# Splitting a vector-matrix product in front of a matmul stage differently: six and two blocks, row form, smaller loads

## The chip, the cores and the metric

The kernel runs on one core of one Trainium2 chip. The metric is the device time of one execution in microseconds (us). Ratios compare the mean time of one kernel's fast runs with that of the other's of the same rounds on the same chip, so they are not quite the ratio of the medians that are quoted. A verdict of faster or slower needs 2%.

## The reference, cut to what matters

The program is one transformer block with conditioning: six vectors come from `silu(c) @ w_mod`, the first two of them (`sa`, a shift, and `ca`, a scale) are needed at once, since they modulate the input of the first projections.

```python
mod = (_silu(c) @ w_mod).reshape(c.shape[0], 6, 1, -1)      # c: 1x1024, w_mod: 1024x6144, bf16
sa, ca, ga, sb, cb, gb = (mod[:, 0], mod[:, 1], ...)         # cut
h = _layernorm(x, axis=-1) * (1 + ca) + sa                   # x: 1x2048x1024
x = x + ga * _A_ref(h, A_wqkv, A_wo)                         # linear attention; k, v, q from h @ wqkv
h = _layernorm(x, axis=-1) * (1 + cb) + sb
x = x + gb * _B_ref(h, B_w_gate, B_w_up, B_w_down)           # gated FFN, F = 3584
```

Of the kernel before, what the change touches and what calls it, by code (L numbers as in the profile page):

```python
# [8 lines left out]
ACT = mybir.ActivationFunctionType  # L9
ALU = mybir.AluOpType  # L10
BF16 = mybir.dt.bfloat16
F32 = mybir.dt.float32
# [9 lines left out]
def kernel(  # L22
# [13 lines left out]
    nc = tc.nc  # L36
    P = nc.NUM_PARTITIONS
    _, S, D = A_x.shape
# [4 lines left out]
    DC = D // P  # L43
# [5 lines left out]
    NB = 512  # L49
# [16 lines left out]
    wm_v = w_mod.rearrange("(j p) n -> p j n", p=P)  # L66
    c_v = c.rearrange("o (j p) -> (o j) p", p=P)

    const = ctx.enter_context(tc.tile_pool(name="const", bufs=1))
# [4 lines left out]
    ep = ctx.enter_context(tc.tile_pool(name="ep", bufs=3))  # L74
# [5 lines left out]
    last_on = {}  # L80
# [16 lines left out]
    def mm(out, lhsT, rhs, start, stop):  # L97
        return tc.keep_in_program_order(nc.tensor.matmul(out, lhsT=lhsT, rhs=rhs, start=start, stop=stop))  # L98

    def transpose(out, in_):  # L100
        return tc.keep_in_program_order(nc.tensor.transpose(out, in_, ident[:]))  # L101

    def big(name, shape):
        return k8.tile([P] + shape, BF16, name=name, tag="k8")
# [4 lines left out]
    def acc_b(name, shape=(NB,), dt=F32):  # L109
        return pb.tile([P] + list(shape), dt, name=name, tag="pb")  # L110
# [3 lines left out]
    c_sb = const.tile([DC, P], BF16, name="c_sb")  # L114
# [3 lines left out]
    def load_x(st, eng):  # L118
        x_sb = k2.tile([P, D], BF16, name="x_sb")
        eng.dma_start(out=x_sb[:], in_=x2[st * P:(st + 1) * P, :])  # L120
        x_tiles[st] = x_sb

    for st in range(STC - 1):
        load_x(st, nc.sync)
    nc.sync.dma_start(out=c_sb[:], in_=c_v)

    wk = [big("wk", [4, D]), big("wk", [4, D])]
    wme = [[big("wme", [DC, NB]) for _ in range(2)] for _ in range(2)]

    def load_mod(b, q, lo, hi):  # L130
        nc.sync.dma_start(out=wme[b][q][:, :, lo:hi], in_=wm_v[:, :, q * D + b * NB + lo:q * D + b * NB + hi])

    def load_k(cc):
        nc.sync.dma_start(out=wk[cc // 4][:, cc % 4, :], in_=wqkv_v[:, cc, D:2 * D])

    load_mod(0, 1, 0, NB)
    load_mod(0, 0, 0, NB)
    load_k(0)
    load_k(1)
    load_x(STC - 1, nc.sync)  # L140
    load_k(2)
    load_k(3)
    load_mod(1, 1, 0, NB)
    load_mod(1, 0, 0, NB // 2)
    load_k(4)
    load_k(5)
    load_mod(1, 0, NB // 2, NB)
    load_k(6)
    load_k(7)

    def load_w(view, lo, name):
        ts = []
# [11 lines left out]
    ident = const.tile([P, P], BF16, name="ident")  # L164
    make_identity(nc, ident[:])
    neg_half = const.tile([P, 1], F32, name="neg_half")
    nc.vector.memset(neg_half[:], -0.5)

    scT = const.tile([P, DC], BF16, name="scT")
    sc32 = const.tile([P, DC, 32], BF16, name="sc32")  # L170

    saT = const.tile([P, DC], F32, name="saT")
    ca1T = const.tile([P, DC], F32, name="ca1T")
    sbT = const.tile([P, DC], F32, name="sbT")
    cb1T = const.tile([P, DC], F32, name="cb1T")
    ga_t = ep.tile([P, NB], F32, name="e")
# [25 lines left out]
    def bn(src, mv_out):  # L202
        stats = small.tile([P, NNB, nc.vector.BN_STATS_DIM], F32, name="stats")
        for i in range(NNB):
            nc.vector.bn_stats(out=stats[:, i, :], in_=src[:, i * NB:(i + 1) * NB])
        nc.vector.bn_aggr(out=mv_out, in_=stats[:])

    def normalise(dst, src, mean, rstd):
        nc.vector.tensor_scalar(out=dst, in0=src, scalar1=mean, scalar2=rstd, op0=ALU.subtract, op1=ALU.mult)
# [7 lines left out]
    def modulate(hT, cc, scaleT, biasT, lo=0, hi=SCW):  # L217
        nc.vector.tensor_scalar(out=hT[:, cc, lo:hi], in0=hT[:, cc, lo:hi], scalar1=scaleT[:, cc:cc + 1],  # L218
                                scalar2=biasT[:, cc:cc + 1], op0=ALU.mult, op1=ALU.add)

    def pe_transpose_tile(hT, xn, t, split):
        tp = acc_b("tp", (DC, P), BF16)
        for cc in range(DC):
            transpose(tp[:, cc, :], xn[:, cc * P:(cc + 1) * P])
        if split < DC:
            nc.scalar.copy(out=hT[:, split:DC, t * P:(t + 1) * P], in_=tp[:, split:DC, :])  # L226
        nc.vector.tensor_copy(out=hT[:, 0:split, t * P:(t + 1) * P], in_=tp[:, 0:split, :])

    hTs = {}

    def ln1_stats(sc, t):
        x_sb = x_tiles.pop(sc * STC + t)
        mv = small.tile([P, STC, 2], F32, name="mv")
        bn(x_sb, mv[:, 0, :])
        rstd = rstd_of(mv, 1)
        return sc, t, x_sb, mv, rstd

    def ln1_norm(sc, t, x_sb, mv, rstd, dve=False):
        xn = k2.tile([P, D], BF16, name="xn", bufs=4)
        if dve:  # L240
            normalise(xn[:], x_sb[:], mv[:, 0, 0:1], rstd[:, 0:1])
        else:
            normalise_act(xn[:], x_sb[:], mv, rstd)
        if sc > 0:
            nc.sync.dma_start_transpose(hTs[sc][:, :, t * P:(t + 1) * P], xn[:])
        return xn
# [3 lines left out]
        for t in range(STC):  # L250
            ln1_norm(*ln1_stats(sc, t))

    def mod_block(b, q, lo, hi):
        for i in range(lo, hi):
            col = q * DC + 4 * b + i
            for j in range(DC):
                mm(mod_ps[:, col:col + 1], lhsT=wme[b][q][:, j, i * P:(i + 1) * P],
                   rhs=scT[:, j:j + 1], start=(j == 0), stop=(j == DC - 1))
        cs = slice(4 * b + lo, 4 * b + hi)
        src = mod_ps[:, q * DC + 4 * b + lo:q * DC + 4 * b + hi]  # L260
        if q == 1:
            nc.vector.tensor_scalar_add(out=ca1T[:, cs], in0=src, scalar1=1.0)
        else:
            nc.vector.tensor_copy(out=saT[:, cs], in_=src)

    last_phi = [None]

# [11 lines left out]
    def k_mms(sc, gs, accs, cc_lo=0, cc_hi=DC):  # L279
        for cc in range(cc_lo, cc_hi):  # L280
            for (t, nb), acc in zip(gs, accs):
                mm(acc[:], lhsT=hTs[sc][:, cc, t * P:(t + 1) * P], rhs=wk[cc // 4][:, cc % 4, nb * NB:(nb + 1) * NB],
                   start=(cc == 0), stop=(cc == DC - 1))
# [129 lines left out]
    def keep_warm(acc, n):  # L413
        for _ in range(n):
            mm(acc[:], lhsT=sel[:, 0, :], rhs=sel[:], start=True, stop=True)

    gs = k_groups[0:6]
    accs = [acc_a() if i < 4 else acc_b("acc") for i in range(6)]
    spare = accs[5]
    keep_warm(spare, 11)  # L420
    hT = hTs[0] = big("hT", [DC, SCW])
    pks[0] = big("pk", [STC, D])
    H = 3 * P
    with in_order(nc.vector, nc.scalar, nc.gpsimd):
        mod_ps = acc_b("mod_ps")
        mm(mod_ps[:, 0:DC], lhsT=c_sb[:], rhs=ident[0:DC, 0:DC], start=True, stop=True)
        keep_warm(spare, 10)
        nc.scalar.activation(out=scT[:], in_=mod_ps[:, 0:DC], func=ACT.Silu)
        xns = [ln1_norm(*ln1_stats(0, t)) for t in range(3)]
        pe_transpose_tile(hT, xns[0], 0, DC)  # L430
        keep_warm(spare, 3)
        pe_transpose_tile(hT, xns[1], 1, DC)
        keep_warm(spare, 2)
        mod_block(0, 1, 0, 4)
        pe_transpose_tile(hT, xns[2], 2, DC // 2)
        keep_warm(spare, 4)
        for lo, hi in ((0, 1), (1, 4)):
            mod_block(0, 0, lo, hi)
            for cc in range(lo, hi):
                modulate(hT, cc, ca1T, saT, 0, H)  # L440
        k_mms(0, gs, accs, 0, 4)
        xn3 = ln1_norm(*ln1_stats(0, 3), dve=True)
        pe_transpose_tile(hT, xn3, 3, DC // 2)
        for cc in range(4):
            modulate(hT, cc, ca1T, saT, H, SCW)
        mod_block(1, 1, 0, 4)
        gs7, accs7 = k_groups[6:7], [acc_b("acc")]
        k_mms(0, gs7, accs7, 0, 2)
        for cc in (4, 5):
            mod_block(1, 0, cc - 4, cc - 3)  # L450
            modulate(hT, cc, ca1T, saT)
            if cc == 4:
                k_mms(0, gs7, accs7, 2, 4)
        k_mms(0, gs + gs7, accs + accs7, 4, 5)
        k_mms(0, gs[0:4], accs[0:4], 5, 6)
        mod_block(1, 0, 2, 4)
        for cc in (6, 7):
            modulate(hT, cc, ca1T, saT)
        k_mms(0, gs[4:6] + gs7, accs[4:6] + accs7, 5, 6)
        k_mms(0, gs + gs7, accs + accs7, 6, 8)  # L460
        gs8, accs8 = k_groups[7:8], [acc_b("acc")]
        k_mms(0, gs8, accs8)
        k_evac(0, gs, accs)
        k_evac(0, gs7, accs7)
        k_evac(0, gs8, accs8)
    with tc.issue_after(last_on[nc.vector.engine]):
        nc.vector.tensor_copy(out=sc32[:], in_=scT[:].unsqueeze(2).to_broadcast([P, DC, 32]))
    with tc.issue_after(last_on[nc.gpsimd.engine]):
        build_masks()

# [219 lines left out]
```

## The kernel before: the parts that the change touches

The columns of h (1024) lie on the 128 partitions in eight blocks (`cc`). Block `cc` of the transposed, normalised x can enter the K matmuls only when its 128 shifts and scales are known. Before the change these come in two stages of four blocks. Each stage is a set of one-column matmuls, with a 128x128 piece of `w_mod` as the stationary operand; each column takes eight of them. "Keep warm" matmuls of zeros fill TensorE while it waits; they are meant to keep its clock up. It is 1.00 in the profile of before from 4.67 us to 40 us.

```python
def load_mod(b, q, lo, hi):            # b: stage, q: 0 shift, 1 scale; 1024 descriptors of 1 KB (or 512 B)
    nc.sync.dma_start(out=wme[b][q][:, :, lo:hi], in_=wm_v[:, :, q * D + b * NB + lo:q * D + b * NB + hi])

load_mod(0, 1, 0, NB); load_mod(0, 0, 0, NB)          # 2 x 1 MB, then
load_k(0); load_k(1); load_x(STC - 1, nc.sync); load_k(2); load_k(3)
load_mod(1, 1, 0, NB); load_mod(1, 0, 0, NB // 2); load_k(4); load_k(5)
load_mod(1, 0, NB // 2, NB); load_k(6); load_k(7)

def mod_block(b, q, lo, hi):
    for i in range(lo, hi):
        col = q * DC + 4 * b + i
        for j in range(DC):
            mm(mod_ps[:, col:col + 1], lhsT=wme[b][q][:, j, i * P:(i + 1) * P],
               rhs=scT[:, j:j + 1], start=(j == 0), stop=(j == DC - 1))
    ...                                               # copy to ca1T (plus 1) or saT on VectorE

# the start, in order on each engine (cut):
mod_block(0, 1, 0, 4); ...; mod_block(0, 0, 0, 1) and (1, 4), modulate(hT, cc, ...) for tiles 0 to 2
k_mms(0, gs, accs, 0, 4)                              # 24 K matmuls, cc 0 to 3, six output groups
xn3 = ln1_norm(*ln1_stats(0, 3), dve=True)            # tile 3 of x
pe_transpose_tile(hT, xn3, 3, DC // 2)
for cc in range(4): modulate(hT, cc, ca1T, saT, H, SCW)
mod_block(1, 1, 0, 4)                                 # 32 one-column matmuls
k_mms(0, gs7, accs7, 0, 2)
...                                                   # mod_block(1, 0, ...) in three pieces among the other K matmuls
```

After the 64 K matmuls of this chunk the wv matmuls follow, and from there TensorE has work to the end.

## Time and profile before

Before the change: 837.79 us median of three runs (837.77, 837.79, 839.96).

From the page of the profiled execution (span, busy time and instructions by engine, the granted TensorE clock in 40 slices, and the chain of waits by engine):

```profile
span 836.6 us, 11355 instructions
...
PE 829.8 (99%) x4701; PEld 380.7 (46%) x4701; DVE 307.6 (37%) x598; ACT 170.1 (20%) x255; POOL 60.9 (7%) x165
...
PEclk9999999999999999999999999999999999999999
...
PE 97%; DMA 1%; DVE 1%; SPq 0%; ACT 0%; issue 0%
```

TensorE (PE) is busy 99% of the span, and the chain that ended last is 97% TensorE work. Only idle or useless TensorE time can be saved, and it lies at the start.

From the timeline of the same run (columns: start in us, length in us, engine, line, operation, tiles, shapes and count; in brackets the idle time before it and what ended that):

```profile
13.30 0.35 PE L98 MATMUL mod_ps<-scT,wme 128*128 128x1 bf16 x8 [0.69 <-DMA wme<-in_w_mod_dram]
...
14.50 5.34 PE L98 MATMUL acc<-wk,hT 128*128 128x512 bf16 x24
...
19.68 0.61 PE L101 MATMUL tp<-ident,xn 128*128 128x128 bf16 x8
...
20.13 0.94 PE L98 MATMUL mod_ps<-scT,wme 128*128 128x1 bf16 x32
...
21.78 0.61 PE L98 MATMUL acc<-wk,hT 128*128 128x512 bf16 x2 [0.71 <-DVE hT L218]
...
31.95 13.98 PE L98 MATMUL acc<-wv,hT 128*128 128x512 bf16 x64
```

One-column matmuls wait for `w_mod` until 13.30, K begins at 14.50 and is broken by the transposes of tile 3, by 32 one-column matmuls, and by 0.71 us of waiting for VectorE at 21.78. The wv matmuls begin at 31.95.

The chain of waits of the same run, in order of time (start, length, what):

```profile
2.98 10.27 DMA wme<-in_w_mod_dram
...
13.30 0.37 PE mod_ps L98 x8
...
13.90 0.74 PE mod_ps L98 x24
```

The second 1 MB block of `w_mod` is what K's start waits for here.

### The profile page before, as it was taken

The numbers are of one execution on the slowest core, as the hardware profiler recorded it, in microseconds if no ns is written. First come the engines' busy times: TensorE is split into PE (matmuls) and PEld (weight loads), VectorE is DVE, ScalarE is ACT, GpSimd is POOL, SyncE is SP. The second block draws the span as 40 slices with busy tenths as digits, with TensorE's granted clock in tenths as the row PEclk, the third lists the DMA queues.
The fourth block names the chain that finished last, engine by engine and source line by source line (L and its number), as shares of the span: only waits on it lengthen the run. The fifth ranks groups of instructions, "written<-read, shape, count | busy, mean of one in ns | idle before, by whom it ended". The sixth has DMA issues, their size and how long they took to land.

```text
span 836.6 us, 11355 instructions
## 1 busy us (share of the span) xinstructions
PE 829.8 (99%) x4701; PEld 380.7 (46%) x4701; DVE 307.6 (37%) x598; ACT 170.1 (20%) x255; POOL 60.9 (7%) x165
## 2 busy tenths in 40 slices
PE   8999999999999999999999999999999999999998
PEld 4444444444444444444444444444444444444444
DVE  5755554587413324521111344222114431111122
ACT  3455343334211111101111110111110101111000
POOL 2011211111130001100000010000001100000000
PEclk9999999999999999999999999999999999999999
DMA  9894890029997446337434173672505529710011
GB/s 311 305 253 100 254 213 2 13 68 239 366 243 262 151 151 207 120 99 229 150 102 151 45 221 100 201 239 62 189 1 127 188 69 322 241 60 0 13 64 51
DMA packets 127668, 129.34 MB, mean 155 GB/s; under 512 B 33920, under 2 KB 109184, under 8 KB 127104
## 3 DMA queue, kind: packets, MB, share of 16 engines
q1 hardware_dynamic: 123568, 115.36, 45.7%
q0 software_dynamic: 4048, 13.25, 5.4%
q8 instruction: 37, 0.61, 0.3%
q14 instruction: 15, 0.12, 0.1%
HBM read 108.53 MB, written 12.72 MB: 145 GB/s over the span
## 4 chain that ended last, share of the span: by engine, by line
PE 97%; DMA 1%; DVE 1%; SPq 0%; ACT 0%; issue 0%
PE acc L98 89%; PE a_ps L98 7%; DMA wme<-in_w_mod_dram 1%; PE kvp L98 1%; PE modr L98 0%; PE den L98 0%; PE mod_ps L98 0%; DVE hT L218 0%; SPq L120 0%; DVE wo L528 0%; PE wf L98 0%; DVE pq L273 0%; ACT eb L270 0%; ACT hT L226 0%; PE tp L101 0%
## 5 line engine op out<-in xcount | busy, mean ns | idle before, releaser
L98 PE MATMUL acc<-h2T,wgu 128*128 128x512 bf16 x1792 | 387.6, 379 | 0.0
L98 PEld LDWEIGHTS <-wgu 128*128 128x128 bf16 x1792 | 175.3, 98 | 211.3
L98 PE MATMUL acc<-wd,gu 128*128 128x512 bf16 (+2 forms) x924 | 196.1, 373 | 0.0
L597 DVE TENSOR_TENSOR gu<-acc,e 128x512 bf16<-128x512 f32 x112 | 77.5, 692 | 299.2 <-PE acc L98 296.5
L596 ACT ACTIVATE e<-acc 128x512 f32<-128x512 f32 x112 | 66.9, 597 | 374.8 <-PE acc L98 374.8
L98 PEld LDWEIGHTS <-gu 128*128 128x128 bf16 x924 | 89.3, 98 | 104.4
L98 PEld LDWEIGHTS <-hT 128*128 128x128 bf16 x512 | 49.2, 98 | 60.4 <-DVE hT L218 1.5
L618 DVE TENSOR_TENSOR e<-acc,gb_bc 128x512 f32<-128x512 f32 (+2 forms) x33 | 22.3, 675 | 131.9 <-PE acc L98 131.9
L98 PE MATMUL acc<-wk,hT 128*128 128x512 bf16 x256 | 57.6, 379 | 0.8 <-DVE hT L218 0.7
L98 PE MATMUL a_ps<-wo,pq 128*128 128x512 bf16 x256 | 57.4, 379 | 0.0
L98 PE MATMUL acc<-hT,wq 128*128 128x512 bf16 x256 | 56.8, 379 | 0.0
L98 PE MATMUL acc<-wv,hT 128*128 128x512 bf16 x256 | 55.9, 379 | 0.0
L270 ACT ACTIVATE eb<-acc 128x512 bf16<-128x512 f32 x64 | 37.9, 595 | 66.2 <-PE acc L98 63.1
L215 ACT ACTIVATE xn<-x,nmr,rstd 128x1024 bf16<-128x1024 f32 x16 | 19.8, 1240 | 126.3 <-POOL nmr L213 126.3
L565 POOL DMA_DIRECT2D x_scratch<-x x16 | 9.7, 608 | 418.5 <-DVE x L558 418.5
L98 PEld LDWEIGHTS <-pq 128*128 128x128 bf16 x256 | 25.0, 98 | 30.2
L98 PEld LDWEIGHTS <-wq 128*128 128x128 bf16 x256 | 24.6, 98 | 29.8 <-issue 0.9
L271 DVE TENSOR_SCALAR eb<-eb 128x512 bf16<-128x512 bf16 x64 | 18.4, 292 | 49.0 <-ACT eb L270 49.0
L558 DVE TENSOR_TENSOR x<-a_ps,x_sb 128x512 f32<-128x512 f32 x32 | 22.1, 691 | 7.9 <-PE a_ps L98 7.8
L199 POOL TENSOR_TENSOR rstd<-veps,neg_half 128x1 f32<-128x1 f32 x32 | 17.9, 559 | 75.3 <-DVE veps L197 72.9
L308 ACT CAST v<-acc 128x512 bf16<-128x512 f32 x32 | 18.3, 582 | 23.1 <-PE acc L98 23.0
L621 DVE TENSOR_TENSOR ob<-e,x1r 128x512 bf16<-128x512 f32 (+2 forms) x33 | 22.3, 675 | 1.0
(70 smaller groups left out, 263.1 us busy)
## 6 DMA issues: line engine op xcount, KB each, us to landing
wgu<-in_B_w_gate_dram SPq DMA_DIRECT2D x28, 1024.0 KB, 7.9
wgu<-in_B_w_up_dram SPq DMA_DIRECT2D x28, 1024.0 KB, 8.7
x_sb<-in_A_x_dram SPq DMA_DIRECT2D x32, 256.0 KB, 6.8
wml<-in_w_mod_dram SPq DMA_DIRECT2D x8, 1024.0 KB, 8.7
x_scratch<-x POOLq DMA_DIRECT2D x16, 512.0 KB, 3.0
x1r<-x_scratch SPq DMA_DIRECT2D x31, 256.0 KB, 2.8
wd<-in_B_w_down_dram SPq DMA_DIRECT2D x7, 1024.0 KB, 6.0
rbc<-rden_scratch POOLq DMA_DIRECT2D x16, 256.0 KB, 5.4
```

Source lines behind the costliest of these rows:

```text
L98: return tc.keep_in_program_order(nc.tensor.matmul(out, lhsT=lhsT, rhs=rhs, start=start, stop=stop))
L199: nc.gpsimd.tensor_tensor(out=rstd[:, 0:n], in0=veps[:, 0:n], in1=neg_half[:].to_broadcast([P, n]), op=ALU.pow)
L215: nc.scalar.activation(out=dst, in_=src, func=ACT.Identity, bias=nmr[:], scale=rstd[:, 0:1])
L270: nc.scalar.activation(out=e[:], in_=acc, func=ACT.Exp)
L271: nc.vector.tensor_scalar(out=e[:], in0=e[:], scalar1=1.0, scalar2=PHI_EPS, op0=ALU.min, op1=ALU.add)
L308: nc.scalar.copy(out=v[:, t * D + nb * NB:t * D + (nb + 1) * NB], in_=acc[:])
L558: nc.vector.tensor_tensor(out=x1[:, ns], in0=a_ps[:], in1=x_t[:, ns], op=ALU.add)
L565: nc.gpsimd.dma_start(out=x1_dram[st * P:(st + 1) * P, :], in_=x1[:])
L596: nc.scalar.activation(out=sg[:], in_=ps[0][:], func=ACT.Silu)
L597: gm = nc.vector.tensor_tensor(out=guT[sc][f // GPT][:, f % GPT, :], in0=ps[1][:], in1=sg[:], op=ALU.mult)
L618: nc.vector.tensor_tensor(out=yt, in0=y_ps, in1=gb_bc[:, ns], op=ALU.mult)
L621: nc.vector.tensor_tensor(out=ob, in0=yt, in1=x1r, op=ALU.add)
```

## The change

Its intent: get six of the eight blocks modulated before K begins, so that K runs nearly unbroken; compute them as rows (`w_mod` streams through and `c` stands still, so that the values come out side by side), on four column tiles of the array (form 128*32 in the traces; 32 such matmuls of 512 columns took 1.91 us in before, 60 ns each, where a K matmul of 512 columns in the form 128*128 takes 216 ns), and turn the rows into columns with VectorE; cut the loads so that none has more than 512 descriptors; put the load of `c` and the first `w_mod` load on ScalarE's queue.

```diff
-    nc.sync.dma_start(out=c_sb[:], in_=c_v)
+    nc.scalar.dma_start(out=c_sb[:], in_=c_v)
...
+    A, MP = 6, 2
+    AW, BW = A * P, (DC - A) * P
+    wma = [big("wme", [MP, 2, AW]) for _ in range(DC // MP)]
+    wmb = big("wme", [DC, 2, BW])
+    def load_a(k, q, eng):                    # 256 descriptors of 1.5 KB
+        eng.dma_start(out=wma[k][:, :, q, :], in_=wm_v[:, k * MP:(k + 1) * MP, q * D:q * D + AW])
+    def load_b(q, lo, hi):                    # 512 descriptors of 512 B
+        nc.sync.dma_start(out=wmb[:, lo:hi, q, :], in_=wm_v[:, lo:hi, q * D + AW:(q + 1) * D])
...
+    for k in range(DC // MP):
+        load_a(k, 1, nc.scalar if k == 0 else nc.sync)
+        load_a(k, 0, nc.sync)
     load_k(0); load_k(1); load_x(STC - 1)     # joined here
+    for cc in range(2, A): load_k(cc)         # joined; then load_b x4, then load_k(6), load_k(7)
...
+    def mod_rows_a(k):
+        for j in range(k * MP, (k + 1) * MP):
+            rows = wma[k][:, j % MP, :, :].rearrange("p q (i r) -> p i q r", r=P)
+            for g in range(4):
+                mm(mod_ps[32 * g:32 * g + 32, 0:A * 64], lhsT=sc32[:, j, :], rhs=rows[:, :, :, 32 * g:32 * g + 32],
+                   start=False, stop=(j == DC - 1))
+    def mod_turn(lo, hi):
+        nc.vector.transpose(out=scr_t[:, lo * 64:hi * 64], in_=mod_ps[:, lo * 64:hi * 64])
...
         # the start
+        nc.vector.tensor_copy(out=sc32[:], in_=scT[:].unsqueeze(2)...)    # was after the K stage; now amid tile 0 and 1
+        mod_rows_a(0) ... mod_rows_a(2); keep_warm(spare, 5); mod_rows_a(3); keep_warm(spare, 4)
+        mod_turn(0, 1); modulate block 0; mod_turn(1, A); modulate blocks 1 to 5
+        k_mms(0, gs, accs, 0, 5)
         xn3 = ...; pe_transpose_tile(hT, xn3, 3); modulate six blocks of tile 3
+        k_mms(0, gs, accs, 5, A)
+        mod_cols_b()                          # 32 one-column matmuls, the two remaining blocks
+        k_mms(0, gs7, accs7, 0, A); modulate blocks 6 and 7; k_mms(0, gs + gs7, accs + accs7, A, DC)
```

Not in this cut: the copies of tiles 2 and 3 out of PSUM go to VectorE alone, and fewer warming matmuls stand at the very start (9 and 6 instead of 11 and 10).

## The prediction

> **What bounds it now.** The page shows TensorE busy 99% of an 836.6 us span. In the view by stretches every one from 28 to 800 us is full but for 0.23 us. So only the start can give time back: whatever moves the end of the first K stage (31.95 us, where the wv matmuls begin) moves the end of the kernel as much.
>
> **The start of before (timeline).** The 64 K matmuls take 216 ns each, 13.9 us. They begin at 14.50 us, 1.23 us after the second 1 MB block of w_mod lands (13.25 us; it heads the chain of waits with 10.27 us). From 14.50 to 31.95 are 17.45 us: 13.9 of K, 0.5 of transposes, about 2.6 of 88 one-column matmuls (24 in 0.74, 32 in 0.94 us), about 0.5 of bubbles at 21-23.5 us.
>
> **What the change does.**
> - One-column matmuls among the K matmuls fall from 88 to 32: 2.6 to 1.0 us. The bubbles mostly go. 17.45 becomes about 15.6.
> - Six of eight blocks become 32 matmuls of 384 columns on column tiles. The same form later in this trace, 32 of 512 columns, took 1.91 us for all, 60 ns each. [...] Only the last eight (0.4 us) follow the last load.
> - Then: turn of 64 columns about 0.22 us (estimate: a 264-column PSUM copy took 0.42, a one-column one 0.16), modulation of 128 columns 0.245. K starts about 1.1 us after the last first-stage load; before, 1.23.
> - Cost: the first stage needs 0.79 MB of x and 3.15 MB of w_mod, not 2.10. Summing before's DMA GB/s by microsecond, 2.88 MB had passed at 10.8 us, yet the block landed at 13.25: the slowest ring lagged 2 us. 3.93 MB had passed at 13.5 us. With 1.5 KB instead of 1 KB descriptors, one load issued by ScalarE (an issue takes 0.4 us), and the same lag or somewhat less from smaller loads, the last lands at 14.8 us (14 to 16). [...] I count no bandwidth from it.
> - VectorE's copies of tiles 2 and 3 (0.69, against 0.58 and 0.42 in series) and the earlier sc32 copy (0.28) are off the path.
>
> **Sum.** K starts at 15.9 us (1.4 later), runs 15.6 us and ends at about 31.4 us: 0.5 to 0.6 earlier. The last wk pieces (same 7.3 MB in all) land near 25 us, when TensorE reaches them, and cost at most a few tenths. Predicted 837.2 us, range 835.7 to 838.6. Chances: faster by over 2% 0.005, within 2% 0.99, slower 0.005.
>
> **What would show each step.** Timeline: last first-stage w_mod load landing at 14-16 us; first K matmul 1.0-1.3 us later; wv matmuls beginning at 30.5-32 us; eight row matmuls in about 0.4 us; no TensorE idle over 0.3 us between them except for wk or the second stage's loads near 22-25 us. After 32 us nothing but the shift.
>
> **What would make it wrong.** Small loads cutting the 2 us lag altogether (K at 14.6: gain 1.8 us); the lag growing with the bytes (K at 17: loss 0.6); second-stage loads, in 512-byte pieces and late in the queue, holding TensorE past 25.4 us; column tiles not overlapping; the clock falling in the longer idle stretches before K.

14.8 us for the last load plus 1.1 is K's start at 15.9, and 15.6 of K put its end at about 31.4, 0.5 to 0.6 earlier than before, so 837.2 us. The 60 ns of a row matmul were measured in before (32 in 1.91 us at 96.72 us), and so was the issue time of 0.4 us (0.38 for `c`, 0.43 for a load of x). The 14.8 us are an estimate from before's bytes and its lag of 2 us; no run at hand then showed what larger descriptors or smaller loads would do to that lag.

## The result, and the profile after

The changed kernel took 838.16 us in the median of four runs (837.71, 837.85, 838.47 and one of 1251.08), the kernel before 838.87 us in the median of its four (837.77 to 839.96). Without the run of 1251 us, the changed kernel's median is 837.85. Executions over 1.5% slower than the fastest of the same kernel are left out of the means. The ratio of the fast runs is 0.999, with an interval of 0.9966 to 1.0013. It falls within 2%, as predicted.

The run of 1251 us is the profiled one. From its page:

```profile
span 1249.2 us, 11163 instructions
...
PEclk7666666666666666666666666666666666666666
```

The clock granted to TensorE is 0.65 from 6.68 us, where the clock record of this trace begins, nearly to the end. None of the other 38 executions of the changed kernel and its variants did this. Nothing below compares it with a run at full clock, and its cause is left open.

So the profile after is that of the first experiment, e1_after, the same kernel run again (836.0 us, clock 1.0). From its page:

```profile
span 836.0 us, 11163 instructions
...
PEclk9999999999999999999999999999999999999999
...
PE 98%; DVE 1%; issue 1%; ACT 0%; POOL 0%
```

Its timeline at the start, against the lines of before shown above:

```profile
5.16 0.18 PE L98 MATMUL mod_ps<-ident,c_sb 8*128 8x8 bf16 x1
...
6.05 0.33 DVE L450 COPY sc<-scT 128x256 bf16<-128x256 bf16 x1 [0.82 <-ACT scT L448]
...
12.94 1.25 PE L98 MATMUL acc<-sel 128*128 128x512 bf16 x5
...
14.12 0.51 PE L98 MATMUL mod_ps<-wme,sc 128*32 128x384 bf16 x8
...
14.68 0.25 DVE L271 STREAM_TRANSPOSE e<-mod_ps 128x64 f32<-128x64 f32 x1 [1.39 <-PE mod_ps L98]
...
15.43 6.64 PE L98 MATMUL acc<-wk,hT 128*128 128x512 bf16 x29
...
23.68 0.94 PE L98 MATMUL mod_ps<-scT,wme 128*128 128x1 bf16 x32
...
30.52 3.83 PE L98 MATMUL acc<-wv,hT 128*128 128x512 bf16 x17
```

K begins at 15.43 (before: 14.50) and wv at 30.52 (before: 31.95). The K stage takes 15.09 us instead of 17.44. The 0.71 us wait at 21.78 is gone, and 33 small matmuls stand in the K stage where 64 stood (the prediction says 88, but 24 of those come before the first K matmul). At the end of the K stage 1.43 us are won. The span is shorter by 0.6 us only. Where the rest went, and how much of the measured difference this is, the experiments have to tell.

The chain of waits of the same run, just before K:

```profile
10.65 1.25 ACT xn L227
11.94 0.62 PE tp L101 x8
12.56 0.44 PE mod_ps L98 x8
13.00 1.19 PE acc L98 x5
14.19 0.44 PE mod_ps L98 x8
```

The wait for `w_mod` that headed the chain before is not in it: K's start now follows from tile 2 of x (normalised by ScalarE until 11.90), its transposes, the third set of row matmuls, five warming matmuls and the last row set.

### The profile page after: what moved, and what is told of

The parts are those of the page before. It is cut to its first block, busy times and chain, and to the rows that moved or that the text cites. A ratio compares the mean times of both kernels' runs of the same rounds, so it can differ in the third digit from the quotient of the medians.

```text
span 1249.2 us, 11163 instructions
## 1 busy us (share of the span) xinstructions
PE 1232.9 (99%) x4560; PEld 468.0 (37%) x4641; DVE 309.5 (25%) x598; ACT 169.3 (14%) x253; POOL 60.8 (5%) x167
## 3 DMA queue, kind: packets, MB, share of 16 engines
q0 software_dynamic: 4048, 13.25, 3.4%
## 4 chain that ended last, share of the span: by engine, by line
PE 99%; issue 1%; DVE 0%
PE acc L98 90%; PE a_ps L98 7%; PE modr L98 0%; PE kvp L98 0%; PE mod_ps L98 0%; PE tp L101 0%; PE den L98 0%; PE wf L98 0%; DVE e L638 0%; DVE ob L641 0%; DVE sel L429 0%; DVE neg_half L172 0%
## 5 line engine op out<-in xcount | busy, mean ns | idle before, releaser
L98 PE MATMUL acc<-h2T,wgu 128*128 128x512 bf16 x1756 | 580.8, 513 | 5.0 <-issue 1.6
L98 PEld LDWEIGHTS <-wgu 128*128 128x128 bf16 x1792 | 217.1, 121 | 367.4 <-issue 367.1
L98 PE MATMUL acc<-wd,gu 128*128 128x512 bf16 (+2 forms) x908 | 293.5, 503 | 2.4 <-issue 1.0
L98 PEld LDWEIGHTS <-gu 128*128 128x128 bf16 x924 | 111.0, 121 | 182.1 <-issue 178.6
L98 PEld LDWEIGHTS <-hT 128*128 128x128 bf16 x512 | 61.6, 121 | 102.9 <-issue 100.6
L98 PE MATMUL a_ps<-wo,pq 128*128 128x512 bf16 x250 | 85.1, 512 | 0.6
L98 PE MATMUL acc<-wk,hT 128*128 128x512 bf16 x248 | 83.7, 513 | 1.3 <-issue 0.8
L98 PE MATMUL acc<-hT,wq 128*128 128x512 bf16 x247 | 83.0, 512 | 1.6 <-issue 1.4
L98 PE MATMUL acc<-wv,hT 128*128 128x512 bf16 x251 | 83.5, 513 | 0.8 <-issue 0.4
L98 PEld LDWEIGHTS <-pq 128*128 128x128 bf16 x256 | 30.8, 120 | 52.6 <-issue 52.6
```

What stands on the lines that cost most here:

```text
L98: return tc.keep_in_program_order(nc.tensor.matmul(out, lhsT=lhsT, rhs=rhs, start=start, stop=stop))
```

## The experiments

Twelve experiments ran, on three chips, all with correct results. Besides the views of the profile I use two readings of the traces' raw records, shown in plain fences: when each of the 16 rings of a load reported its share landed, and the 16,384-byte packets of the instruction queue. A load is one entry of the list of DMA issues; "late ring" means the last ring's landing against the first one's. Loads that share a semaphore with the eight-ring load of `c` cannot be read this way and are left out.

### e1_after: the changed kernel again

Edit: none.

> The changed kernel again, for a profile at full clock and an interval. Both theories: last first-stage w_mod load lands at about 13.6 us (as in the profile taken at the low clock, which had no late ring), first K matmul at 14.7, K stage 15.6 us long, wv matmuls from about 30.3 us. Theory LAG (loads of 1024 descriptors make one ring late in the kernel before): before's runs are all late alike, so this is 1.2 to 1.7 us faster than every run of before, ratio about 0.998. Theory STRAY (a chance stall of one packet made the ring late in the one profile of before): some runs of before are as fast as this or faster, and this gains under 0.5 us on those.

Measured: 837.66 us (837.31 to 837.87, five runs); before in the same rounds 839.07 (837.94 to 839.85, nine runs); ratio 0.9985 (0.9971 to 0.9998). The last first-stage load landed at 13.57 as expected, K started 0.7 us later than expected, wv began at 30.52. Both times of before that theory STRAY asked for are there: some runs of before are within 0.3 us of this kernel, others 1.5 us above it.

The records of the runs give the mean granted clock, and it separates them. Over the four sets of rounds the kernel before ran 45 times: 27 times at a clock of 1.000, mean 838.09 us (837.52 to 838.96), and 18 times at 0.998, mean 839.56 us (839.05 to 841.02). The changed kernel's eight fast runs all have 0.999 or 1.000, mean 837.76 us. So there are two differences: 0.33 us against the good runs of before, and 18/45 of 1.47 us, or 0.59 us, because before loses clock in two of five runs. Together 0.92 us. The 45 runs come from three chips; on the chip and in the rounds of this experiment alone the first difference is 0.50 us (838.12 in eight runs of before at full clock, 837.61 here).

### e2_before: the kernel before again

Edit: none.

> The kernel before, unchanged, for a second profile and for the noise of the ratio (1.000 expected). LAG: the last ring of the first w_mod blocks lands 2.3 to 2.9 us after the median ring again, K from about 14.5 us. STRAY: the spread over the rings is about 0.6 us this time, the second block lands at about 11.2 us, K from about 12.4 us and wv matmuls from under 31 us.

Measured: 837.95 us (837.71 to 839.27, one run of five at clock 0.998); ratio to the other runs of the same kernel 0.9992 (0.998 to 1.0005), which is the noise to bear in mind. The late ring came again:

```
last first-stage w_mod load that can be read: first, median, last ring landed (us)   last minus first
before      1024 descriptors   10.44  10.89  13.25   2.81
e2_before   1024               10.63  11.07  13.06   2.43
e5_c_act    1024               10.70  11.45  13.11   2.41
e9_warm     1024               10.64  10.77  13.47   2.83
e10_warm2   1024               10.55  11.34  12.67   2.12
e3_small     256                9.84  10.95  11.21   1.37
e4_sp        256               12.56  12.91  13.78   1.22
e6_c_sp      256               13.05  13.23  14.16   1.11
e7_count     256               13.05  13.45  13.90   0.85
e11_best     256               13.02  13.44  13.78   0.76
e13_cols     256               13.10  13.41  13.81   0.71
e12_wml      256               13.07  13.29  13.62   0.55
e1_after     256               13.06  13.28  13.57   0.51
```

It is not a chance event: every profile with loads of 1024 descriptors has it at 2.1 to 2.8 us, every one with 256 at 0.5 to 1.4 (1.1 to 1.4 with `c` on SyncE's queue, 0.5 to 0.9 with `c` on ScalarE's). STRAY falls as an account of the late ring. In before it is not one ring but five of the sixteen, landing at 12.12 to 13.25. And the lag is not tied to these loads: the `wk` load behind these `w_mod` loads, with 128 descriptors, has 2.81 us in before as well, and in e5_c_act the third load of x, issued before any `w_mod` load, already has 2.49. Bytes went along with the number of descriptors (1 MB against 0.25 to 0.4 MB), so which of the two counts is not shown. What makes a ring late at all was not found.

### e3_small: the kernel before with small loads alone

```diff
-        nc.sync.dma_start(out=wme[b][q][:, :, lo:hi], in_=wm_v[:, :, ...])
+        for j in range(0, DC, 2):
+            nc.sync.dma_start(out=wme[b][q][:, j:j + 2, lo:hi], in_=wm_v[:, j:j + 2, ...])
```

> The kernel before with each w_mod load cut in four along j (256 descriptors each), nothing else. LAG: the second block lands at 11.2 us instead of 13.25, K starts about 2 us earlier, the time falls by 1 to 2 us. STRAY: no different from the kernel before of the same rounds (within 0.3 us in the fastest runs).

Measured: 839.3 us (838.01 to 839.67; three of five at clock 0.998), before 839.07; ratio 1.0003 (0.999 to 1.0015). The lag halved, as LAG says, and K began at 13.89 instead of 14.50, yet no time was won, against LAG: its two runs at full clock took 838.39 us on average, those of before in the same rounds 838.12. Its profile is one of the runs that lost clock (half from 22.73 to 26.14 us), so only what lies ahead of 22.73 can be compared. The chain of waits there:

```profile
13.29 6.25 DMA wme<-in_w_mod_dram
...
19.56 2.31 DMA wme<-in_w_mod_dram
...
21.89 0.35 PE mod_ps L98 x8
```

The chain runs through loads of the second stage's `w_mod` to 21.87, and TensorE stands idle for 0.34 us on them, a wait that before does not have there. So in before's order of loads 0.34 of the 0.61 us by which K starts earlier are lost again to the second stage; where the rest goes this profile can't show. Small loads gained no time by themselves there.

### e4_sp: the changed kernel with both loads back on SyncE's queue

```diff
-    nc.scalar.dma_start(out=c_sb[:], in_=c_v)
+    nc.sync.dma_start(out=c_sb[:], in_=c_v)
-        load_a(k, 1, nc.scalar if k == 0 else nc.sync)
+        load_a(k, 1, nc.sync)
```

> The changed kernel with its c load and its first w_mod load back on SyncE's queue. If ScalarE's queue buys issue time alone, the last first-stage load lands at most 0.4 us later and the time rises by 0 to 0.4 us. If the second queue adds bandwidth at the start or keeps a ring from falling behind, it lands 1 to 2 us later and the time rises as much.

Measured: 838.64 us (837.95 to 838.96), mean 838.50 against 837.61 for e1_after in the same rounds: 0.9 us slower, more than the issue time of 0.4 us that the expectation allowed for. K began at 16.20 and wv at 31.29, both 0.77 us later. But it was not the `w_mod` loads that did it. From the timeline:

```profile
6.12 0.09 PEld L98 LDWEIGHTS <-c_sb 8*128 8x128 bf16 x1 [1.84 <-DMA c_sb<-in_c_dram]
...
6.84 0.29 DVE L450 COPY sc<-scT 128x256 bf16<-128x256 bf16 x1 [1.71 <-ACT scT L448]
```

TensorE waits for `c` until 6.12. In e1_after it took `c` up at 5.16, after its warming matmuls and with no wait for the load; VectorE's copy of `sc32` then began at 6.05, here at 6.84. The change has put that copy between the statistics of tile 0 and those of tile 1, and VectorE ran them in that order in both traces (in the chains of waits the statistics of tile 1 follow at 6.37 and 7.13), so a late `c` delayed tiles 1 and 2, and these head the chain to K.

### e5_c_act: the kernel before with `c` on ScalarE's queue

```diff
-    nc.sync.dma_start(out=c_sb[:], in_=c_v)
+    nc.scalar.dma_start(out=c_sb[:], in_=c_v)
```

> The kernel before with only its load of c moved from SyncE's to ScalarE's queue. Theory C (the 2 KB load of c between the x and the w_mod loads in one queue makes some rings late): the late rings go, the spread of the rings on the first two w_mod blocks falls from 2.4-2.8 to about 0.6 us, the second block lands at about 11.3 us, K starts near 12.6 us, and the time falls by up to 1.5 us. Theory W (what helps is the first w_mod load on a second queue): spread and time as in the kernel before.

Measured: 838.85 us (837.48 to 840.04; three of six at clock 0.998), before 838.31; ratio 1.0002 (0.9989 to 1.0015). The late ring stays (2.41 us), K at 14.36. Theory C, that the small load of `c` makes the ring late, falls. Its profile caught the low clock, which is used below.

### e6_c_sp: the changed kernel with `c` alone back on SyncE's queue

```diff
-    nc.scalar.dma_start(out=c_sb[:], in_=c_v)
+    nc.sync.dma_start(out=c_sb[:], in_=c_v)
```

> The changed kernel with only its load of c moved back to SyncE's queue; the first w_mod load stays on ScalarE's. C: spread of 1.2 us or more on the first-stage loads, as with both on SyncE's (last landing near 14.5 us), and 0.5 to 1 us slower than the changed kernel. W: spread 0.5 us, last landing at 13.6 us, time as the changed kernel.

Measured: 838.74 us (838.51 to 839.06), before 838.31; ratio 1.0001. That is 1.2 us above e1_after's mean, though on another chip. The spread is 1.1 us and the last landing 14.16, near what C expected, but as e5 took C down, I read this otherwise: TensorE waits for `c` until 6.39 (2.06 us of idle weight loading before it, ended by that load), `sc32` follows at 7.10, K at 16.47 and wv at 31.55, each about 1.04 us later than in e1_after. So on the queue side the useful part of the change is that `c` comes early. Theory W falls too: with the first `w_mod` load still on the second queue, the spread is 1.11 us and not 0.5, and the last landing is no earlier than with both loads on SyncE's queue (13.78 in e4_sp).

### e7_count: the changed kernel with TensorE's stream as long as before

```diff
     def keep_warm(acc, n):
         for _ in range(n):
-            mm(acc[:], lhsT=sel[:, 0, :], rhs=sel[:], start=True, stop=True)
+            for lo, hi in ((0, 1), (1, 3), (3, 4)):
+                mm(acc[:, lo * P:hi * P], lhsT=sel[:, 0, :], rhs=sel[:, lo:hi, :], start=True, stop=True)
+    for _ in range(2):
+        mm(spare[:, 0:1], lhsT=sel[:, 0, :], rhs=sel[:, 0, 0:1], start=True, stop=True)
```

Before this run I had looked for the time that the changed kernel gives back. From the first wv matmul to the last are 117.96 us in before and e2_before, but 118.67 in e1_after. The timeline at 60 to 70 us of before:

```profile
63.12 1.22 PE L98 MATMUL kvp<-v,pk 128*32 128x64 bf16 x128
...
64.27 6.00 PE L98 MATMUL acc<-wk,hT 128*128 128x512 bf16 x27
```

and of e1_after:

```profile
61.69 1.22 PE L98 MATMUL kvp<-v,pk 128*32 128x64 bf16 x128
...
62.85 2.55 PE L98 MATMUL acc<-wk,hT 128*128 128x512 bf16 x10
...
65.95 4.26 PE L98 MATMUL acc<-wk,hT 128*128 128x512 bf16 x19 [0.55 <-issue]
```

After the 128 small kv matmuls (256 rows of the stream with their weight loads) and ten K matmuls TensorE stops for 0.55 us, and what ended it is called "issue", nothing that the profile shows. In the traces the instruction queue carries packets of 16,384 bytes, 37 in before and 36 in e1_after (queue q8 of their pages), for 9402 and 9282 rows of TensorE's stream (matmuls and weight loads; 9404 and 9284 by my count of the program): 254 and 258 rows for each. From this I estimate that each packet is a block of about 256 rows of that stream, so that a stream of another length meets its block boundaries at other places of the work.

> The changed kernel with each warming matmul cut in three by columns (and two small ones more), so that TensorE's stream is as long as before (9404 rows, not 9284) and blocks of instructions are fetched at the same places of the work as before. Theory FETCH (the 0.55 us stop at 65.9 us is TensorE waiting for a 16 KB block of instructions that the w_mod loads of that moment delay): the stop goes, blocks are fetched at about 17, 27, 49 and 65 us, and the span falls by about 0.5 us. Theory SUPPLY (the earlier start runs into some other wait there): the stop stays.

Measured: 837.03 us (836.85 to 837.20), before 838.31 (837.72 to 839.84, eleven runs); ratio 0.998 (0.9968 to 0.9992). The stop is gone, in its timeline:

```profile
62.69 7.51 PE L98 MATMUL acc<-wk,hT 128*128 128x512 bf16 x34
```

From the first wv matmul to the last are 117.96 us again, and wv begins at 30.36. The 16 KB packets of the instruction queue began at 13.84, 27.39, 47.85 and 63.52 us; in before at 17.40, 27.92, 50.37 and 65.99; in e1_after at 17.15, 34.79, 63.31 and 67.06. This is what FETCH expected, and SUPPLY falls, though the first of the four packets came 3 us before the expected time. A second sign, from traces already at hand: in the three full-clock profiles with the short stream and these loads, the stop ends 2.63 or 2.64 us after the packet of a block began (63.31 and 65.95 in e1_after, 64.13 and 66.76 in e4_sp, 64.21 and 66.84 in e6_c_sp). This version is 1.1 us below the full-clock runs of before in its rounds (838.09), and its slowest run is below the fastest of e1_after, which ran on another chip.

### e12_wml: the changed kernel with the loads at 54 to 66 us moved

```diff
-            if sc == 1:
-                blks = mod_load([2 * D, 2 * D + NB, 5 * D, 5 * D + NB])      # before v_phase(sc)
...
+        if sc == 1:                                                          # after v_phase(sc) and ln1(sc + 1)
+            blks = mod_load([2 * D, 2 * D + NB, 5 * D, 5 * D + NB])
```

> The changed kernel, stream of 9284 rows, with the four 1 MB w_mod loads that are under way at 54-66 us asked for after the v stage of the second chunk instead of before it, so that the DMA rings carry little at 57-66 us. If the stop of TensorE at 65.9 us is a block fetch held up by those loads, the stop goes. If it comes from two block boundaries close together at the 256 small kv matmuls, whatever the rings carry, it stays at 0.4-0.6 us.

Measured: 838.59 us (837.47 to 841.68, four runs, the slowest at clock 0.998), before 838.96; ratio 1.0003 (0.9982 to 1.0023). The move costs time elsewhere, so the time says nothing here (TensorE has a new stop of 0.34 us at 109.6). The window does: with the short stream and the rings empty there is no stop.

```profile
62.67 7.51 PE L98 MATMUL acc<-wk,hT 128*128 128x512 bf16 x34
```

The DMA queues from 60 to 66 us (packets, MB, share of the rings) in e1_after:

```profile
q1 hardware_dynamic: 1477, 1.48, 77.4%
q8 instruction: 1, 0.02, 1.2%
```

and in e12_wml, where the queue of data carried nothing in this window:

```profile
q8 instruction: 2, 0.03, 2.3%
```

Two blocks start in these 6 us in e12_wml, at 60.01 and 63.78, the first 1.5 us ahead of the kv matmuls (61.52); in e1_after, with the same stream, they start at 63.31 and 67.06, 3.3 us later, of which 0.17 us is TensorE's own delay (its kv matmuls begin at 61.69). So in these runs the stop came with two things together, the short stream and data loads in the rings at that moment (e1_after, e4_sp, e6_c_sp); with either one taken away (e7_count, e12_wml) it was gone. That the short stream matters because it puts a block boundary just ahead of the kv matmuls, which run through 256 rows in 1.22 us, is my estimate from these times, not shown.

### e9_warm and e10_warm2: the low clock of before

The low clock comes in one stretch of 3.41 us at half the clock. The profiles of e5_c_act and e3_small have it (23.04 to 26.45 and 22.73 to 26.14 us). The view by stretches, with boundaries at the steps in its clock record (stretch, its length, TensorE busy time and matmuls, granted clock, DMA share, GB/s), of e5_c_act:

```profile
19.63:23.04 3.41, 2.58 (x55) 1.00 1.10 372
23.04:26.45 3.41, 3.35 (x17) 0.50 1.05 404
```

and the same stretches of before, which was profiled at full clock:

```profile
19.63:23.04 3.41, 2.58 (x53) 1.00 1.12 353
23.04:26.45 3.41, 3.34 (x38) 1.00 1.05 392
```

The dip of e5_c_act begins 17.07 us after its clock record does (5.97 us), five times its own length within 0.02 us. So I read the records in windows of that length, counted from their first step; that what happens in such a window sets the clock of the next one is an assumption, not shown. In e5_c_act and in before TensorE is busy 2.58 of 3.41 us from 19.63 on, at least 40 one-column matmuls among it. Counted so, the windows of before's profile begin elsewhere (its record of full clock begins at 4.67 us, that of e5_c_act at 5.97), which would be why it escaped; this is not shown. Busy time alone does not decide: counted from the first step of their clock records, e2_before has a window with 2.29 us (20.74 to 24.15, about 1% of its matmul records missing) and e9_warm one with 2.00 (21.38 to 24.79), and neither lost clock after it. What sets the two windows ahead of a dip apart is the number of columns that the matmuls starting in them stream: 1968 in e3_small and 2858 in e5_c_act. In the 13 profiles but that of the slow run, no other such window up to about 34 us has under 3100. Two dips are no test of that. The idea to test: fill that place.

First try, e9_warm:

```diff
         mod_block(1, 1, 0, 4)
+        for _ in range(3):
+            mm(mod_ps[:, P:NB], lhsT=sel[:, 0, :], rhs=sel[:, 1:4, :], start=True, stop=True)
         gs7, accs7 = ...
```

> The kernel before with three idle matmuls of 384 columns (0.5 us) in the 0.7 us in which TensorE waits at 21 us. Theory CLOCK (about half of the runs of before lose 3.4 us at half clock just after 21-23 us, where TensorE's activity is low, and read a mean clock of 0.998 and 1.2 us more): no run, or one of five, at 0.998; median about 838.0 instead of 839.1. Otherwise: the same mix of 0.998 and 1.000 as before, 10 of 24 runs.

The "10 of 24" of this text was a miscount: the records then showed 6 of 14 for before. Measured: 839.52 us (838.26 to 839.88; two of five at 0.998); ratio 1.0007 (0.9995 to 1.0019). The edit missed its aim, as its timeline shows:

```profile
22.72 0.65 PE L98 MATMUL mod_ps<-sel 128*128 128x384 bf16 x3 [1.44 <-DVE ca1T L262]
```

The filling matmuls write `mod_ps`, which VectorE was to read, waited for that read (1.44 us, ended by VectorE's `ca1T`), and made the idle time longer (0.71 us in before). Second try, e10_warm2, with four of them ahead of the one-column matmuls, where no read is pending:

```diff
+        for _ in range(4):
+            mm(mod_ps[:, P:NB], lhsT=sel[:, 0, :], rhs=sel[:, 1:4, :], start=True, stop=True)
         mod_block(1, 1, 0, 4)
```

> The clock test again; in the first try the idle matmuls themselves waited for VectorE's read of mod_ps and made the idle time longer. Now four idle matmuls of 384 columns (0.65 us) stand before the 32 one-column matmuls at 20 us, where nothing is pending on mod_ps; they end before VectorE is done with tile 3, so they should delay nothing. CLOCK: none or one of five runs at a mean clock of 0.998 (before: 10 of 25), median 838.0 or less. Otherwise 2 or 3 of five at 0.998, and the window of low activity is not what sets off the slow clock.

Measured: 837.95 us (837.68 to 838.11), before 838.96 (837.52 to 841.02, eleven runs, five at 0.998); ratio 0.9989 (0.9975 to 1.0003). None of the five runs at 0.998. The same stretches of its profile:

```profile
19.63:23.04 3.41, 3.23 (x61) 1.00 1.11 354
23.04:26.45 3.41, 3.34 (x31) 1.00 1.06 396
```

With 0.65 us of zeros, at no cost (the K stage is 17.44 us as before), before takes 837.95, about the time of the changed kernel. Five runs without a dip, where two in five have one, could be luck with a chance of 8%, so the clock is strongly indicated, not proven, as what the filling changed. That the dips are what separates the two groups of before's runs is shown by their clock.

### e11_best: fewer warming matmuls before K

```diff
-        keep_warm(spare, 5)
+        keep_warm(spare, 3)
```

on top of e7_count, with six more one-column matmuls at the very start.

> The changed kernel with TensorE's stream as long as before (as in e7_count), and three warming matmuls instead of five ahead of the last eight row matmuls (their small pieces are made up for elsewhere). If those warming matmuls held up the K start (in one profile the last load had landed at 13.57 us and the row matmuls began at 14.12), K starts up to 0.4 us earlier than 15.3 us: 836.7 us, against 837.0 for e7_count and 838.2 to 839.1 for the kernel before. If the load is what holds it up, 837.0 us.

Measured: 837.5 us (836.90 to 837.67), before 838.96; ratio 0.9982 (0.9968 to 0.9996). Not faster than e7_count's 837.03 (on another chip; before at full clock averaged 838.09 there and 838.10 here). The row matmuls began at 13.90 instead of 14.12, but K began at 15.67:

```profile
15.67 1.02 PE L98 MATMUL acc<-wk,hT 128*128 128x512 bf16 x4 [0.28 <-DMA wk<-in_A_wqkv_dram]
```

It now waited for the first piece of `wk`. This piece's last ring was 1.99 us behind its first, where the load just before it had 0.76. A 16 KB block of instructions had started at 13.44 us and taken 1.01 us. In e1_after the same packet starts at 17.15, and the loads around it go from 0.48 to 1.66 us of lag. My expectation had left out that loads may land later beside such a packet; these two pairs are all that shows it.

### e13_cols: six blocks as columns again, in the new order

```diff
-        mod_rows_a(k)                  # four times
+        mod_cols_a(k)                  # 24 one-column matmuls on wma[k], accumulated over k in mod_ps[:, 0:2 * A]
-        mod_turn(0, 1); ...; mod_turn(1, A); ...
+        nc.vector.tensor_copy(out=sca[:, :, 0:A], in_=mod_ps[:, 0:2 * A].rearrange("p (q i) -> p q i", q=2))
```

> The changed kernel with its six first-stage blocks computed as one-column matmuls (96 in all, 24 after the last load) as before, in the new order of loads and stages; no turn on VectorE. TensorE's stream then has 9406 rows, about as many as before. Theory ROW (the row form on column tiles is what makes the change pay): the last 24 take about 0.7 us instead of 0.5 and K starts 0.3 us later than 15.3 us or more; time as the kernel before. Theory ORDER (what pays is the new split and order of the loads and stages; the row form and the turns do not matter): K starts within 0.3 us of 15.3 us, wv at 30.3 to 30.7 us, and, as the stream has its old length, no stop at 66 us: 837.0 us, as e7_count and below the changed kernel's 837.7.

Measured: 837.22 us (837.15 to 837.51), before 838.16 (837.83 to 839.65, nine runs); ratio 0.9988 (0.9974 to 1.0002). Its timeline:

```profile
13.72 0.74 PE L98 MATMUL mod_ps<-scT,wme 128*128 128x1 bf16 x24
...
14.50 0.17 DVE L469 COPY sca<-mod_ps 128x12 f32<-128x12 f32 x1 [1.57 <-PE mod_ps L98]
...
15.19 6.64 PE L98 MATMUL acc<-wk,hT 128*128 128x512 bf16 x30
...
30.27 1.03 PE L98 MATMUL acc<-wv,hT 128*128 128x512 bf16 x4
```

The last 24 one-column matmuls take 0.74 us instead of 0.51 for eight rows, but a copy of 0.17 us replaces the turn of 0.25, and K starts at 15.19, no later than with rows. The K stage takes 15.08 us, as in the changed kernel. ORDER holds, ROW falls: the row form and the turns bring nothing here. As the stream is long again (9406 rows), there is no stop at 66 us either. This kernel keeps the split, the order, the small loads and the early `c` together, so it does not tell these apart.

## Why the prediction was right or wrong

Time and class were right: 837.2 predicted, range 835.7 to 838.6, measured 838.16 (837.85 without the slow run) and 837.66 in two sets. The gain over before was predicted as 0.6 us; the medians say 0.7 (1.0 without the slow run) and 1.4, the means of all fast runs 0.9. But it is right by errors that offset one another: that the number came so close is luck. The table takes the profiles at full clock, from before to e1_after; each line is a difference of times in these two traces. The pair is one of each: K starts at 14.50 in before but at 14.32 in e2_before, so a few tenths are noise, and over many runs the difference at full clock was 0.33 to 0.50 us.

| term | predicted | measured |
|---|---|---|
| start of K | +1.4 us (15.9) | +0.93 (15.43) |
| length of the K stage | -1.8 (to 15.6) | -2.35 (17.44 to 15.09) |
| after the K stage | 0 | +0.81 (0.71 from first to last wv, where the stop is, and 0.1 after) |
| sum | -0.5 | -0.61 (the spans: 836.6 and 836.0) |
| low clock in two of five runs of before | not seen | -0.59 on average |

- **What bounds it now: right.** Only the start counts, and every difference of K's end moves the whole. e7_count and e13_cols show it: the 117.96 us from first to last wv are the same in all nine profiles whose stream is about as long as before's.
- **The K stage: right in mechanism, mis-sized.** It takes 15.09 us, not 15.6, as no bubble at all is left. Two terms were off in opposite directions. The prediction let one-column matmuls fall from 88 to 32 and save 1.6 us; inside the stage they fall from 64 to 33, from 1.88 to 0.83 us (start to start, in before and in e7_count, whose stage is as long as e1_after's). But idle time fell from 0.94 us to nothing, where about 0.5 had been counted, and the K matmuls, no longer broken up, from 14.17 to 13.81. 15.08 or 15.09 came out in all seven kernels with the new order, and 17.43 or 17.44 in the three of the old order whose clock and order were undisturbed.
- **"the last lands at 14.8 us (14 to 16)": wrong, 13.57.** The lag of a ring was carried over at nearly 2 us; with the smaller loads it is 0.5. The prediction had named this as a risk.
- **"K starts about 1.1 us after the last first-stage load": wrong, 1.86.** The load is not on the chain. The row matmuls wait behind five warming matmuls until 14.12, and these behind tile 2 of x, whose statistics come after the `sc32` copy that I called off the path. e4_sp and e6_c_sp show the price of that place: 0.77 and 1.04 us for a late `c`.
- **"After 32 us nothing but the shift": wrong.** A stop of 0.55 us came, 0.71 us in all between first and last wv, which was gone with the old stream length (e7_count) and with empty rings (e12_wml). A count of rows would have been enough to suspect it.
- **"I count no bandwidth from it" (the load on ScalarE's queue): right as far as it goes, but too little.** The second queue is not seen to save anything in the `w_mod` loads (last landing 13.78 us with both loads on SyncE's queue in e4_sp, 14.16 with `c` alone there in e6_c_sp), but it took `c` out of the queue behind x: TensorE waited for `c` until 6.12 and 6.39 us in those two, and not at all in e1_after.
- **The clock.** I looked for a fall in the idle stretches of the changed kernel before K; there was none in e1_after (clock 1.0, waits of 0.35 and 0.57 us for ScalarE). The one that matters was in before (clock 0.998 in 18 of 45 runs); where a profile caught it, in e5_c_act, it came after a stretch recorded as mostly busy (2.58 of 3.41 us), and it could have been guessed from 837.8 and 839.96 in its times.

## What to carry to other kernels

Before pricing a change to a well filled kernel, look at the spread of its own runs and at their granted clocks: here two fifths of them lost 1.5 us at a mean clock of 0.998, which none of five runs did once four dummy matmuls filled a thin place. When a change alters the number of instructions on a busy engine, look for new "issue" stops after the place of the change, here 0.55 us soon after 256 short rows had run in 1.22 us beside large loads, and try the old stream length. And take a change with several parts apart: here the new split and order of loads and stages, with `c` early, brought the gain, and the row form brought nothing. The small loads brought nothing by themselves in the old order; no run has the new order with large loads, so their share in it is open.

Left open: why rings fall behind, and whether the number of descriptors or the size of a load counts; what exactly sets off the half clock; how a block boundary comes to stop TensorE; the run at clock 0.655; and whether taking `c` up before the nine first warming matmuls, which now head the chain, would bring K forward.
